# A feed-forward kernel: no plain feature tile, eighteen early P2 products, seven products for every tile

## The chip, the cores and the metric

The kernel runs on one core of one Trainium2 chip. Times are device microseconds (us) of that core. The engines are TensorE (PE: matmuls; PEld: its weight loads), VectorE (DVE), ScalarE (ACT), GpSimd (POOL) and the issuing queue of SyncE (SPq). SBUF and PSUM are the two memories on the core that the engines work on; the matmuls here write into PSUM, in banks. A "matmul" below is one instruction with a 128x128 stationary and a 128x512 moving operand, unless said otherwise.

## The reference

```
B, S, D, F = 32, 32, 1024, 3584          # 1024 tokens, bf16 throughout
def reference(x, w_gate, w_up, w_down):
    return (gelu_tanh(x @ w_gate) * (x @ w_up)) @ w_down
```

## The kernel before

The 3584 features are 28 feature tiles of 128, in 14 chunks of two. For one feature tile, the gate and up weights, each cut into the two halves of D, form a 2x2 block matrix (a11, a12: gate; a21, a22: up), and x transposed forms another (b11, b12: first half of D, tokens 0-511 and 512-1023; b21, b22: second half of D). A plain tile needs eight block products of four matmuls, 32 in all. Chunks 1 to 13 use a scheme of seven products (28 matmuls), which needs sums of blocks: s1 to s4 of the weights, per chunk, and t1 to t4 of x, once. The products P1 = a11 b11 and P2 = a12 b21 stay bf16; the other five multiply sums in fp32r, a 32-bit type. The last step of a tile is the gating product: VectorE multiplies gelu of the gate result by the up result.

- Before, chunk 0 is plain. Its 64 matmuls need no sums, and they fill PE while x arrives and VectorE forms the t's and the sums of chunk 1.
- P2 of ten further tiles is also made in the head ("ahead") from gate weights that arrive first, and kept in SBUF.
- GpSimd makes the sums of chunks 2 to 13. It starts when t4 is done.

```python
# head, before (cut)
for k in range(KQ):
    for j in range(KB):
        product_ahead(ps[j], 0, j, k, k + 1)      # P2 of tiles 2..5
plain0(KD, KD + KQ)                               # plain, tokens 0-511
...
tt(t1, b12, b11, SUB)                             # VectorE
for fl in range(FC):
    for which in (0, 1):
        plain(tok0[fl][which], which, fl, 0, 0, KD, KD, KD - 1)
    plain_out(fl, 0, *tok0[fl])
...
tt(t2, b22, t1, SUB)
chunk1 = sums(1, nc.vector)                       # s1, s2, s4 of chunk 1
...                                               # plain, tokens 512-1023
begun = [first_product(FC + fl) for fl in range(FC)]   # P1 of chunk 1

# one chunk (cut): order of the products on PE
for fl in range(FC): prod(psc[fl], s1[fl], t1, True);  sn5.append(snap(psc[fl], "sn5"))
for fl in range(FC): prod(psa[fl], s2[fl], t2, False); sn2.append(snap(psa[fl], "sn2"))
for st in open_fts:  last_product(st)             # a22 t4 of the chunk before; its gating
                                                  # product on VectorE frees that psA bank
for fl, ft in enumerate(fts):
    prod(psc[fl], s4[fl], b22r, False)
    h1.append(gelu(added(sn2[fl], psc[fl]), "h1", 2))   # this add frees the psC bank
begun = [first_product(ft + FC) for ft in fts]    # P1 of the next chunk, new psA banks
for fl, ft in enumerate(fts):
    prod(psa[fl], s3[fl], t3, False)
    tt(g_of(ft)[:, NB:], added(sn5[fl], psa[fl]), h1[fl], MUL)
```

`snap` copies a bank to SBUF on ScalarE, `added` adds on VectorE. There are eight PSUM banks: four psA, two psB, two psC.

Of the kernel before, what the change touches and what calls it, by code (L numbers as in the profile page):

```python
# [1 line left out]

# [11 lines left out]
def kernel(  # L14
# [20 lines left out]
    nc = tc.nc  # L35
    P = nc.NUM_PARTITIONS
# [14 lines left out]
    FC = 2  # L51
    NCH = FT // FC
    NAHEAD = 10
    KQ = DT // 4
# [12 lines left out]
    gpool = ctx.enter_context(tc.tile_pool(name="g", bufs=1))  # L67
    ring = ctx.enter_context(tc.tile_pool(name="ring", bufs=4))
    one = ctx.enter_context(ExitStack())
# [38 lines left out]

    a12_ahead = [ring.tile([P, KD, KB * P], bf16, name="a12a", tag="ring") for _ in range(2)]
    b11 = xpool.tile([P, KD, NB], bf16, name="b11")  # L110
    b21 = xpool.tile([P, KD, NB], bf16, name="b21")
    b12 = ring.tile([P, KD, NB], bf16, name="b12", tag="ring")
    b22 = ring.tile([P, KD, NB], bf16, name="b22", tag="ring")
    t1, t2, t3, t4, b22r = (xpool.tile([P, KD, NB], f32r, name=n) for n in ("t1", "t2", "t3", "t4", "b22r"))

    def x_rows(dt, nb):
        return ((b11, b12), (b21, b22))[dt // KD][nb][:, dt % KD, :]


    ahead = [  # L120
        gpool.tile([P, n, NB], fp32, name="ahead", tag=f"hi{n}", bufs=2) for n in (KB, KB, QF - KB)
    ]
    assert 2 * KB < NAHEAD <= KB + QF
    w_tiles = {}
# [15 lines left out]
    def quads(ci, fl=None):  # L140
        cols = slice(None) if fl is None else slice(fl * P, (fl + 1) * P)
        wg, wu = w_tiles[ci, 0], w_tiles[ci, 1]
        return wg[:, :KD, cols], wg[:, KD:, cols], wu[:, :KD, cols], wu[:, KD:, cols]

    s_tiles = {}

    def sums(ci, eng):

        a11, a12, a21, a22 = quads(ci)
        s1, s2, s4, s3 = (  # L150
            spool.tile([P, KD, FC * P], f32r, name=n, tag=n) for n in ("s1", "s2", "s4", "s3")
        )
        s_tiles[ci] = (s1, s2, s3, s4)
        yield eng.tensor_tensor(s1, a21, a22, ADD)  # L154
        yield eng.tensor_tensor(s2, s1, a11, SUB)  # L155
        yield eng.tensor_tensor(s4, a12, s2, SUB)  # L156
        yield eng.tensor_tensor(s3, a11, a21, SUB)  # L157

# [16 lines left out]
    with tc.manual_schedule():  # L175
        for eng, p0, p1 in ((nc.sync, 0, HALF), (nc.scalar, HALF, NB_P)):
# [3 lines left out]
            )  # L180
        alloc_w(0, 0)
        alloc_w(0, 1)

        def load_ahead(i, k0, k1):
            f0, n = FC + i * KB, min(KB, NAHEAD - i * KB)
            nc.sync.dma_start(  # L186
                out=a12_ahead[i][:, k0:k1, : n * P],
                in_=wg_r[:, KD + k0 : KD + k1, f0 * P : (f0 + n) * P],
            )

        def load_w0(eng, d0, d1):
            for which in (0, 1):
                load_w(eng, 0, which, d0, d1)

# [6 lines left out]
        for k in range(KQ):  # L201
            load_ahead(0, k, k + 1)
        load_w0(nc.scalar, KD, KD + KQ)
        load_xT(0, KD + KQ, DT)
        load_ahead(0, KQ, KD)
        load_w0(nc.sync, KD + KQ, DT)
        load_ahead(1, 0, KD)
        load_xT(0, 0, KD)
        load_w0(nc.sync, 0, KD)
        load_xT(1, 0, KD)  # L210
        load_xT(1, KD, DT)

        warm_ps = acc("A")
# [14 lines left out]

        def plain(ps, which, fl, nb, d0, d1, first=0, last=DT - 1):
            for dt in range(d0, d1):  # L230
                nc.tensor.matmul(  # L231
                    ps,
                    lhsT=w_tiles[0, which][:, dt, fl * P : (fl + 1) * P],
                    rhs=x_rows(dt, nb),
                    start=(dt == first),
                    stop=(dt == last),
                )

        def gelu(src, tag, bufs):
            h = ework.tile([P, NB], bf16, name=tag, tag=tag, bufs=bufs)  # L240
            nc.scalar.activation(h, src, ACT.Gelu_apprx_tanh)  # L241
            return h

        def plain_out(ft, nb, gate, up):
            tt(g_of(ft)[:, nb * NB : (nb + 1) * NB], gelu(gate, "h0", 4), up, MUL)  # L245

# [10 lines left out]

        def ahead_of(ft):
            i, j = divmod(ft - FC, KB)
            return ahead[i][:, j, :]  # L260

        def product_ahead(ps, i, j, k0=0, k1=KD):
            for k in range(k0, k1):
                nc.tensor.matmul(  # L264
                    ps,
                    lhsT=a12_ahead[i][:, k, j * P : (j + 1) * P],
                    rhs=b21[:, k, :],
                    start=(k == 0),
                    stop=(k == KD - 1),
                )  # L270


        ps = [acc(t) for t in "CCAA"]
        tok0 = [(acc("A"), acc("B")) for _ in range(FC)]

        def plain0(d0, d1):
            for which in (0, 1):
                for dt in range(d0, d1):
                    for fl in range(FC):
                        plain(tok0[fl][which], which, fl, 0, dt, dt + 1, KD, KD - 1)  # L280

        for k in range(KQ):
            for j in range(KB):
                product_ahead(ps[j], 0, j, k, k + 1)
        plain0(KD, KD + KQ)
        for j, copy in enumerate((nc.scalar.copy, nc.vector.tensor_copy) * 2):
            product_ahead(ps[j], 0, j, KQ)
            copy(ahead[0][:, j, :], ps[j])
        plain0(KD + KQ, DT)
        a12_ahead.append(ring.tile([P, KD, KB * P], bf16, name="a12a", tag="ring"))  # L290
        load_w_all(1, 1)
        load_w_all(1, 0)
        load_ahead(2, 0, KD)
        load_w_all(2, 0)
        for j, tag in enumerate("CCAA"):
            ps = acc(tag)
            product_ahead(ps, 1, j)
            (nc.scalar.copy, nc.vector.tensor_copy)[j % 2](ahead[1][:, j, :], ps)
        tt(t1, b12, b11, SUB)
        for fl in range(FC):  # L300
            for which in (0, 1):
                plain(tok0[fl][which], which, fl, 0, 0, KD, KD, KD - 1)
            plain_out(fl, 0, *tok0[fl])
        tok1 = [(acc("A"), acc("B")) for _ in range(FC)]
        for fl in range(FC):
            for which in (0, 1):
                plain(tok1[fl][which], which, fl, 1, 0, KD)
        tt(t2, b22, t1, SUB)
        nc.scalar.copy(b22r, b22)
        chunk1 = sums(1, nc.vector)  # L310
        for _ in range(3):
            next(chunk1)
        for fl in range(FC):
            for which in (0, 1):
                plain(tok1[fl][which], which, fl, 1, KD, DT)
            plain_out(fl, 1, *tok1[fl])
        load_w_all(2, 1)
        for j, tag in enumerate("CC"):
            ps = acc(tag)
            product_ahead(ps, 2, j)  # L320
            nc.scalar.copy(ahead[2][:, j, :], ps)

# [11 lines left out]
        def first_product(ft):  # L334
            psa = acc("A")
            prod(psa, quads(*divmod(ft, FC))[0], b11, True)
            if ft < FC + NAHEAD:
                return psa, gelu(added(ahead_of(ft), psa), "h0", 4)
            return psa, snap(psa, "sn1")
# [5 lines left out]

        tt(t3, b22, b12, SUB)
        begun = [first_product(FC + fl) for fl in range(FC)]
        next(chunk1)
# [3 lines left out]
        open_fts = []  # L352
        for ci in range(1, NCH):
            fts = range(ci * FC, (ci + 1) * FC)
            if fts[0] == HF:
                g_hi = g_tiles("hi", bf16, N)
            if ci + 1 < NCH:
                if ci + 2 < NCH:
                    load_w_all(ci + 2, 0)
                for _ in sums(ci + 1, nc.gpsimd):  # L360
                    pass
# [7 lines left out]
            for fl in range(FC):  # L369
                prod(psa[fl], s2[fl], t2, False)  # L370
                sn2.append(snap(psa[fl], "sn2"))
            for st in open_fts:
                last_product(st)
            for fl, ft in enumerate(fts):
                prod(psc[fl], s4[fl], b22r, False)
                h1.append(gelu(added(sn2[fl], psc[fl]), "h1", 2))
                a22r_of(ft)
            if ci + 2 < NCH:
                load_w_all(ci + 2, 1)

            if fts[0] < FC + NAHEAD:
                h0 = first
            else:
                for fl in range(FC):
                    psb = acc("B")
                    prod(psb, quads(ci, fl)[1], b21, True)
                    h0.append(gelu(added(first[fl], psb), "h0", 4))
            begun = [first_product(ft + FC) for ft in fts] if ci + 1 < NCH else []
            for fl, ft in enumerate(fts):
                prod(psa[fl], s3[fl], t3, False)  # L390
                tt(g_of(ft)[:, NB:], added(sn5[fl], psa[fl]), h1[fl], MUL)  # L391
            open_fts = list(zip(fts, psa, h0))

# [5 lines left out]
        NBT = len(batches)  # L399

        def load_b(f_off, col, b, t=None):
            k0, k1 = batches[b]
            if t is None:
                t = ring.tile([P, KB, NB], bf16, name="wdb", tag="ring")[:, : k1 - k0, :]
            nc.sync.dma_start(
                out=t, in_=wd_r[:, f_off + k0 : f_off + k1, col * NB : (col + 1) * NB]
            )
            return t
# [173 lines left out]
```

## Time and profile before

| | before |
|---|---|
| time, median of the 6 runs beside the result | 275.59 us |
| span of the profiled run | 273.7 us |
| PE busy | 269.1 us (98%) |
| PE idle after its start | one wait, 0.15 us |
| granted TensorE clock | 1.00 |
| last x quadrant (b22) landed (issue 14.89 + 4.2) | 19.1 us |
| first s1 product of chunk 2 | 38.54 us |

The first two lines are of the profile page: busy time of each engine, then the mean granted clock in 40 slices of the span (tenths; 9 is 90% or more), then the chain that ended last, by engine.

```profile
PE 269.1 (98%) x1199; PEld 187.9 (69%) x1199; DVE 195.9 (72%) x194; ACT 111.9 (41%) x183; POOL 107.3 (39%) x55
...
PEclk9999999999999999999999999999999999999999
...
PE 91%; SPq 5%; DMA 2%; issue 0%; DVE 0%; ACT 0%; DVEq 0%
```

The list of waits of PE (engine, line, what it waited for, us in total, times, longest):

```profile
PE psA L215 <- PEq L566: 0.8, 1, 0.8
PE psB L231 <- DVE lo L245: 0.2, 1, 0.2
```

PE is the limit from end to end, and it never waits for a load. The timeline of PE (start, duration, operation; bf16 products last about 1.73 us for eight matmuls from start to start, fp32r ones 1.815) at the end of the head and the beginning of chunk 2:

```profile
27.74 1.89 PE L249 MATMUL psA<-b,wg 128*128 128x512 bf16 x8
29.28 2.21 PE L249 MATMUL psC<-t,s 128*128 128x512 f32 x8
...
36.51 2.19 PE L249 MATMUL psA<-t,s 128*128 128x512 f32 x8
38.54 1.98 PE L249 MATMUL psC<-t,s 128*128 128x512 f32 x8
```

### The profile page before, as it was taken

Reading aid. Unit: us, or ns where it says so; the run is one execution under the profiler, and the core shown is the slowest. Engines: PE = TensorE matmul, PEld = TensorE weight load, DVE = VectorE, ACT = ScalarE, POOL = GpSimd, SP = SyncE. Lnnn points to the kernel's source line nnn. Section 1 sums busy time; section 2 is a strip of 40 time slices with the busy share of each in tenths; the row PEclk is TensorE's granted clock in tenths of the full one; section 3 lists DMA queues with packets and bytes.
Section 4 is the critical chain, followed back from the end, with each engine's and each line's share of the span. In section 5 each row is a group of like instructions: output and inputs, shape, how many; then the busy total and the mean of one; then the engine's idle time right before and its main releaser. Section 6 shows DMA issues by size and latency. Waiting matters only on the chain.

```text
span 273.7 us, 3347 instructions
## 1 busy us (share of the span) xinstructions
PE 269.1 (98%) x1199; PEld 187.9 (69%) x1199; DVE 195.9 (72%) x194; ACT 111.9 (41%) x183; POOL 107.3 (39%) x55
## 2 busy tenths in 40 slices
PE   8999999999999999999999999999999999999994
PEld 3444777877778676676868686754447888888883
DVE  0279986989756676676657556568999999999511
ACT  2262664553643646455563636430300023962001
POOL 1000099998797695949576675000000000000000
PEclk9999999999999999999999999999999999999999
DMA  7997532513505405050504280004992445686202
GB/s 175 267 245 198 152 104 50 156 54 102 156 8 145 135 18 153 3 153 0 156 25 130 67 282 0 0 2 161 353 292 79 116 153 172 230 279 202 78 0 78
DMA packets 55810, 35.08 MB, mean 128 GB/s; under 512 B 8689, under 2 KB 55793, under 8 KB 55793
## 3 DMA queue, kind: packets, MB, share of 16 engines
q1 hardware_dynamic: 52672, 32.38, 41.1%
q10 hardware_dynamic: 3120, 2.49, 2.7%
q8 instruction: 9, 0.15, 0.2%
q14 instruction: 9, 0.07, 0.1%
HBM read 30.93 MB, written 2.10 MB: 121 GB/s over the span
## 4 chain that ended last, share of the span: by engine, by line
PE 91%; SPq 5%; DMA 2%; issue 0%; DVE 0%; ACT 0%; DVEq 0%
PE psA L249 34%; PE psA L412 18%; PE psC L249 17%; PE psC L412 7%; PE psB L412 7%; PE psB L249 5%; SPq L197 3%; DMA b<-in_x_dram 2%; PE psB L231 1%; PE psA L231 1%; SPq L134 1%; SPq L186 1%; PE psC L264 1%; DVE lo L245 0%; ACT o_sb L552 0%
## 5 line engine op out<-in xcount | busy, mean ns | idle before, releaser
L249 PE MATMUL psA<-t,s 128*128 128x512 f32 x208 | 54.1, 402 | 0.0
L241 ACT ACTIVATE h<-c 128x512 bf16<-128x512 f32 x52 | 31.8, 628 | 37.2 <-DVE c L326 37.2
L249 PEld LDWEIGHTS psA<-t,s 128*128 128x128 f32 x208 | 39.1, 188 | 9.2
L154 POOL TENSOR_TENSOR s<-wu 128x1024 fp32r<-128x1024 bf16 x12 | 26.4, 2202 | 25.0 <-DMA wu<-in_w_up_dram 18.3
L326 DVE TENSOR_TENSOR c<-sn,psA 128x512 f32<-128x512 f32 x26 | 17.8, 683 | 16.8 <-PE psA L249 16.8
L249 PEld LDWEIGHTS <-wg 128*128 128x128 bf16 x168 | 15.4, 98 | 20.1 <-issue 3.4
L155 POOL TENSOR_TENSOR s<-s,wg 128x1024 fp32r<-128x1024 f32 x12 | 27.8, 2313 | 0.9
L156 POOL TENSOR_TENSOR s<-wg,s 128x1024 fp32r<-128x1024 bf16 x12 | 26.3, 2188 | 0.9
L157 POOL TENSOR_TENSOR s<-wg,wu 128x1024 fp32r<-128x1024 bf16 x12 | 26.6, 2213 | 0.0
L331 ACT COPY sn<-psC 128x512 f32<-128x512 f32 x26 | 15.2, 588 | 27.6 <-PE psC L249 23.8
L331 ACT COPY sn<-psA 128x512 f32<-128x512 f32 x42 | 23.6, 585 | 6.8 <-PE psA L249 6.8
L249 PE MATMUL psC<-t,s 128*128 128x512 f32 x104 | 25.9, 391 | 0.0
L249 PE MATMUL psA<-t,a22r 128*128 128x512 f32 x104 | 25.9, 391 | 0.0
L249 PE MATMUL psC<-b22r,s 128*128 128x512 f32 x104 | 25.7, 389 | 0.0
L249 PE MATMUL psA<-b,wg 128*128 128x512 bf16 x104 | 24.6, 380 | 0.0
L249 PEld LDWEIGHTS psC<-t,s 128*128 128x128 f32 x104 | 19.5, 188 | 4.2
L249 PEld LDWEIGHTS psA<-t,a22r 128*128 128x128 f32 x104 | 19.5, 188 | 4.1
L249 PEld LDWEIGHTS psC<-b22r,s 128*128 128x128 f32 x104 | 19.5, 188 | 4.1
L326 DVE TENSOR_TENSOR c<-sn,psC 128x512 f32<-128x512 f32 x26 | 17.9, 689 | 5.3 <-PE psC L249 5.3
L391 DVE TENSOR_TENSOR lo<-c,h 128x512 bf16<-128x512 f32 x12 | 19.2, 1602 | 0.6
L344 DVE TENSOR_TENSOR hi<-h,psA 128x512 bf16<-128x512 bf16 x14 | 9.6, 688 | 13.8 <-PE psA L249 13.8
L455 ACT COPY snb<-psC 128x512 f32<-128x512 f32 x4 | 2.2, 590 | 36.5 <-PE psC L412 36.5
(93 smaller groups left out, 402.6 us busy)
## 6 DMA issues: line engine op xcount, KB each, us to landing
wu<-in_w_up_dram SPq DMA_DIRECT2D x13, 512.0 KB, 4.0
wg<-in_w_gate_dram SPq DMA_DIRECT2D x13, 512.0 KB, 5.2
wdb<-in_w_down_dram SPq DMA_DIRECT2D x12, 512.0 KB, 4.7
wdb<-in_w_down_dram SPq DMA_DIRECT2D x12, 384.0 KB, 4.2
v<-in_w_down_dram SPq DMA_DIRECT2D x4, 512.0 KB, 6.2
out_dram<-o_sb ACTq DMA_DIRECT2D x16, 128.0 KB, 1.7
v<-in_w_down_dram SPq DMA_DIRECT2D x4, 384.0 KB, 7.5
a12a<-in_w_gate_dram SPq DMA_DIRECT2D x2, 256.0 KB, 5.9
```

Of the source, the lines that this page charges most:

```text
L154: yield eng.tensor_tensor(s1, a21, a22, ADD)
L155: yield eng.tensor_tensor(s2, s1, a11, SUB)
L156: yield eng.tensor_tensor(s4, a12, s2, SUB)
L157: yield eng.tensor_tensor(s3, a11, a21, SUB)
L197: nc.sync.dma_start_transpose(out=t[:, d0 % KD : (d1 - 1) % KD + 1, :], in_=xf[nb * NB : (nb + 1) * NB, d0 * P : d1 * P])
L241: nc.scalar.activation(h, src, ACT.Gelu_apprx_tanh)
L249: nc.tensor.matmul(ps, lhsT=lhs[:, k, :], rhs=rhs[:, k, :], start=(start and k == 0), stop=(k == KD - 1), skip_group_check=True,)
L326: tt(t, s, ps, ADD)
L331: nc.scalar.copy(t, ps)
L344: tt(g_of(ft)[:, :NB], h0, psa, MUL)
L391: tt(g_of(ft)[:, NB:], added(sn5[fl], psa[fl]), h1[fl], MUL)
L412: nc.tensor.matmul(banks[m], lhsT=lhs(k)[:, m * P : (m + 1) * P], rhs=rhs(k), start=(start and k == 0), stop=(k == HF - 1), skip_group_che ...
```

## The change

The intent is to drop the plain chunk: 56 matmuls in place of 64 for its two tiles. Something else must then fill PE while x and the first weights arrive, so P2 of eighteen tiles, not ten, is made in the head. The extra results are kept in SBUF slots that are needed later only. VectorE makes all sums of chunk 0 and s1 of chunk 1, GpSimd the rest. Because P1 of chunk 0 goes on accumulating in its bank before VectorE has time, ScalarE copies it to SBUF, and the add P1 + P2 of chunk 0 is put off into chunk 1.

```diff
-    NAHEAD = 10
+    NAHEAD = 18
-        load_w0(nc.sync, KD + KQ, DT)
-        load_ahead(1, 0, KD)
-        load_xT(0, 0, KD)
-        load_w0(nc.sync, 0, KD)
-        load_xT(1, 0, KD)
+        load_ahead(nc.sync, 1, KQ, KD)
+        load_ahead(nc.sync, 2, 0, KD)
+        load_xT(0, 0, KD)
+        load_ahead(nc.sync, 3, 0, KD)
+        load_xT(1, 0, KD)                 # b12
+        load_ahead(nc.sync, 4, 0, KD)
+        load_w_all(0, 1)                  # up weights of chunk 0
         load_xT(1, KD, DT)                # b22
+        load_w(nc.sync, 0, 0, 0, KD)      # gate weights of chunk 0, first half
 ... (plain0, plain, plain_out and their calls removed)
+        for ft in range(NAHEAD): ... product_ahead(ps, ft); copy(ahead[ft], ps)
+        chunk0 = sums(0, [nc.vector] * 4)
         tt(t1, b12, b11, SUB)
+        next(chunk0)                      # s1
         tt(t2, b22, t1, SUB)
+        next(chunk0); next(chunk0)        # s2, s4
+        tt(t3, b22, b12, SUB)
+        next(chunk0)                      # s3
-            if ft < FC + NAHEAD:
-                return psa, gelu(added(ahead_of(ft), psa), "h0", 4)
+            if FC <= ft < NAHEAD:
+                return psa, gelu(added(ahead[ft], psa), "h0", 4)
             return psa, snap(psa, "sn1")
-        for ci in range(1, NCH):
+        for ci in range(NCH):
+            if ci == 1:
+                open_fts = [(ft, ps, gelu(added(ahead[ft], p1), "h0", 4)) for ft, ps, p1 in open_fts]
             for st in open_fts:
                 last_product(st)
```

(The loop also loads the gate weights of chunk 2 a second time.)

More of the change, by code (lines that the diff above doesn't have):

```diff
@@ L1 @@
 from contextlib import ExitStack
+from itertools import cycle
 import concourse.bass as bass
@@ L67 @@
     gpool = ctx.enter_context(tc.tile_pool(name="g", bufs=1))
-    ring = ctx.enter_context(tc.tile_pool(name="ring", bufs=4))
+    ring = ctx.enter_context(tc.tile_pool(name="ring", bufs=2))
     one = ctx.enter_context(ExitStack())
@@ L105, in acc, with a12_tile @@
         return ps1.tile([P, NB], fp32, name=f"ps{tag}", tag=tag, bufs=BANKS[tag])
-    a12_ahead = [ring.tile([P, KD, KB * P], bf16, name="a12a", tag="ring") for _ in range(2)]
+    def a12_tile(pool, tag):
+        return pool.tile([P, KD, KB * P], bf16, name="a12a", tag=tag)
+    a12_ahead = [
+        a12_tile(*at) for at in ((spool, "s3"), (ring, "ra"), (ring, "ra"), (spool, "s2"), (spool, "s4"))
+    ]
     b11 = xpool.tile([P, KD, NB], bf16, name="b11")
     b21 = xpool.tile([P, KD, NB], bf16, name="b21")
-    b12 = ring.tile([P, KD, NB], bf16, name="b12", tag="ring")
-    b22 = ring.tile([P, KD, NB], bf16, name="b22", tag="ring")
+    b12 = ring.tile([P, KD, NB], bf16, name="b12", tag="rb")
+    b22 = ring.tile([P, KD, NB], bf16, name="b22", tag="rb")
     t1, t2, t3, t4, b22r = (xpool.tile([P, KD, NB], f32r, name=n) for n in ("t1", "t2", "t3", "t4", "b22r"))
@@ L117, in x_rows, with ahead_tile @@
         return ((b11, b12), (b21, b22))[dt // KD][nb][:, dt % KD, :]
-    ahead = [
-        gpool.tile([P, n, NB], fp32, name="ahead", tag=f"hi{n}", bufs=2) for n in (KB, KB, QF - KB)
-    ]
-    assert 2 * KB < NAHEAD <= KB + QF
+    def ahead_tile(pool, n, tag):
+        t = pool.tile([P, n, NB], fp32, name="ahead", tag=tag, bufs=2)
+        return [t[:, j, :] for j in range(n)]
+    ahead = [a for n in (KB, KB, QF - KB, QF - KB) for a in ahead_tile(gpool, n, f"hi{n}")]
     w_tiles = {}
@@ L142, in quads @@
         wg, wu = w_tiles[ci, 0], w_tiles[ci, 1]
-        return wg[:, :KD, cols], wg[:, KD:, cols], wu[:, :KD, cols], wu[:, KD:, cols]
+        a12 = wg[:, KD:, cols] if ci else a12_ahead[0][:, :, : FC * P][:, :, cols]
+        return wg[:, :KD, cols], a12, wu[:, :KD, cols], wu[:, KD:, cols]
     s_tiles = {}
@@ L153, in sums @@
         s_tiles[ci] = (s1, s2, s3, s4)
-        yield eng.tensor_tensor(s1, a21, a22, ADD)
-        yield eng.tensor_tensor(s2, s1, a11, SUB)
-        yield eng.tensor_tensor(s4, a12, s2, SUB)
-        yield eng.tensor_tensor(s3, a11, a21, SUB)
+        yield eng[0].tensor_tensor(s1, a21, a22, ADD)
+        yield eng[1].tensor_tensor(s2, s1, a11, SUB)
+        yield eng[2].tensor_tensor(s4, a12, s2, SUB)
+        yield eng[3].tensor_tensor(s3, a11, a21, SUB)
     a22rs = {}
@@ L180, with load_ahead @@
             )
-        alloc_w(0, 0)
-        alloc_w(0, 1)
-        def load_ahead(i, k0, k1):
-            f0, n = FC + i * KB, min(KB, NAHEAD - i * KB)
-            nc.sync.dma_start(
+        def load_ahead(eng, i, k0, k1):
+            f0, n = i * KB, min(KB, NAHEAD - i * KB)
+            eng.dma_start(
                 out=a12_ahead[i][:, k0:k1, : n * P],
@@ L189, in load_ahead @@
             )
-        def load_w0(eng, d0, d1):
-            for which in (0, 1):
-                load_w(eng, 0, which, d0, d1)
         def load_xT(nb, d0, d1):
@@ L201 @@
         for k in range(KQ):
-            load_ahead(0, k, k + 1)
-        load_w0(nc.scalar, KD, KD + KQ)
+            load_ahead(nc.sync, 0, k, k + 1)
+            load_ahead(nc.scalar, 1, k, k + 1)
         load_xT(0, KD + KQ, DT)
-        load_ahead(0, KQ, KD)
-        load_w0(nc.sync, KD + KQ, DT)
-        load_ahead(1, 0, KD)
+        load_ahead(nc.sync, 0, KQ, KD)
+        load_ahead(nc.sync, 1, KQ, KD)
+        load_ahead(nc.sync, 2, 0, KD)
         load_xT(0, 0, KD)
-        load_w0(nc.sync, 0, KD)
+        load_ahead(nc.sync, 3, 0, KD)
         load_xT(1, 0, KD)
+        load_ahead(nc.sync, 4, 0, KD)
+        load_w_all(0, 1)
         load_xT(1, KD, DT)
+        alloc_w(0, 0)
+        load_w(nc.sync, 0, 0, 0, KD)
+        load_w_all(1, 1)
+        load_w_all(1, 0)
+        load_w_all(2, 0)
         warm_ps = acc("A")
@@ L227 @@
         nc.tensor.matmul(warm_ps[:, : NB // 2], lhsT=ones_w, rhs=ones_m[:, : NB // 2], start=True, stop=True)
-        def plain(ps, which, fl, nb, d0, d1, first=0, last=DT - 1):
-            for dt in range(d0, d1):
-                nc.tensor.matmul(
-                    ps,
-                    lhsT=w_tiles[0, which][:, dt, fl * P : (fl + 1) * P],
-                    rhs=x_rows(dt, nb),
-                    start=(dt == first),
-                    stop=(dt == last),
-                )
         def gelu(src, tag, bufs):
@@ L242, in gelu @@
             return h
-        def plain_out(ft, nb, gate, up):
-            tt(g_of(ft)[:, nb * NB : (nb + 1) * NB], gelu(gate, "h0", 4), up, MUL)
         def prod(ps, lhs, rhs, start):
@@ L256, in prod, with product_ahead @@
                 )
-        def ahead_of(ft):
-            i, j = divmod(ft - FC, KB)
-            return ahead[i][:, j, :]
-        def product_ahead(ps, i, j, k0=0, k1=KD):
+        def product_ahead(ps, ft, k0=0, k1=KD):
+            i, j = divmod(ft, KB)
             for k in range(k0, k1):
@@ L270, in product_ahead @@
                 )
-        ps = [acc(t) for t in "CCAA"]
-        tok0 = [(acc("A"), acc("B")) for _ in range(FC)]
-        def plain0(d0, d1):
-            for which in (0, 1):
-                for dt in range(d0, d1):
-                    for fl in range(FC):
-                        plain(tok0[fl][which], which, fl, 0, dt, dt + 1, KD, KD - 1)
-        for k in range(KQ):
-            for j in range(KB):
-                product_ahead(ps[j], 0, j, k, k + 1)
-        plain0(KD, KD + KQ)
-        for j, copy in enumerate((nc.scalar.copy, nc.vector.tensor_copy) * 2):
-            product_ahead(ps[j], 0, j, KQ)
-            copy(ahead[0][:, j, :], ps[j])
@@ L289 @@
-        plain0(KD + KQ, DT)
-        a12_ahead.append(ring.tile([P, KD, KB * P], bf16, name="a12a", tag="ring"))
-        load_w_all(1, 1)
-        load_w_all(1, 0)
-        load_ahead(2, 0, KD)
-        load_w_all(2, 0)
-        for j, tag in enumerate("CCAA"):
-            ps = acc(tag)
-            product_ahead(ps, 1, j)
-            (nc.scalar.copy, nc.vector.tensor_copy)[j % 2](ahead[1][:, j, :], ps)
-        tt(t1, b12, b11, SUB)
-        for fl in range(FC):
-            for which in (0, 1):
-                plain(tok0[fl][which], which, fl, 0, 0, KD, KD, KD - 1)
-            plain_out(fl, 0, *tok0[fl])
@@ L304 @@
-        tok1 = [(acc("A"), acc("B")) for _ in range(FC)]
-        for fl in range(FC):
-            for which in (0, 1):
-                plain(tok1[fl][which], which, fl, 1, 0, KD)
+        head = [acc(t) for t in "CCBBAAAA"]
+        for q in range(2):
+            for k in range(KQ):
+                for ft in range(q * KB, (q + 1) * KB):
+                    product_ahead(head[ft], ft, k, k + 1)
+        for ft in range(NAHEAD):
+            if ft < 2 * KB:
+                ps = head[ft]
+                product_ahead(ps, ft, KQ)
+            else:
+                ps = acc("CCBBAAAA"[ft % 8])
+                product_ahead(ps, ft)
+            if ft == len(ahead):
+                ahead += ahead_tile(ring, 2, "ra")
+            (nc.vector.tensor_copy if ft % 3 == 1 and ft < 3 * KB else nc.scalar.copy)(ahead[ft], ps)
@@ L308 @@
+        chunk0 = sums(0, [nc.vector] * 4)
+        tt(t1, b12, b11, SUB)
+        next(chunk0)
         tt(t2, b22, t1, SUB)
         nc.scalar.copy(b22r, b22)
-        chunk1 = sums(1, nc.vector)
-        for _ in range(3):
-            next(chunk1)
-        for fl in range(FC):
-            for which in (0, 1):
-                plain(tok1[fl][which], which, fl, 1, KD, DT)
-            plain_out(fl, 1, *tok1[fl])
+        next(chunk0)
+        next(chunk0)
+        tt(t3, b22, b12, SUB)
+        next(chunk0)
@@ L317 @@
         load_w_all(2, 1)
-        for j, tag in enumerate("CC"):
-            ps = acc(tag)
-            product_ahead(ps, 2, j)
-            nc.scalar.copy(ahead[2][:, j, :], ps)
         def added(s, ps):
@@ L344, in last_product @@
             tt(g_of(ft)[:, :NB], h0, psa, MUL)
-        tt(t3, b22, b12, SUB)
-        begun = [first_product(FC + fl) for fl in range(FC)]
+        begun = [first_product(fl) for fl in range(FC)]
+        chunk1 = sums(1, (nc.vector, nc.gpsimd, nc.gpsimd, nc.gpsimd))
         next(chunk1)
@@ L359 @@
                     load_w_all(ci + 2, 0)
-                for _ in sums(ci + 1, nc.gpsimd):
+                for _ in chunk1 if ci == 0 else sums(ci + 1, [nc.gpsimd] * 4):
                     pass
@@ L377 @@
                 a22r_of(ft)
-            if ci + 2 < NCH:
+            if 0 < ci < NCH - 2:
                 load_w_all(ci + 2, 1)
-            if fts[0] < FC + NAHEAD:
+            if 0 < fts[0] < NAHEAD:
                 h0 = first
-            else:
+            elif ci:
                 for fl in range(FC):
@@ L391 @@
                 tt(g_of(ft)[:, NB:], added(sn5[fl], psa[fl]), h1[fl], MUL)
-            open_fts = list(zip(fts, psa, h0))
+            open_fts = list(zip(fts, psa, h0 or first))
         A11, A12 = [[g[:, :, :NB] for g in gs] for gs in (g_hi, g_lo)]
@@ L399 @@
         NBT = len(batches)
+        ring_tags = cycle(("ra", "rb"))
         def load_b(f_off, col, b, t=None):
@@ L403, in load_b @@
             if t is None:
-                t = ring.tile([P, KB, NB], bf16, name="wdb", tag="ring")[:, : k1 - k0, :]
+                t = ring.tile([P, KB, NB], bf16, name="wdb", tag=next(ring_tags))[:, : k1 - k0, :]
             nc.sync.dma_start(
```

## The prediction

> **What bounds it now.** TensorE: the page has PE busy 98% of 273.7 us, the chain of waits is 91% PE, and the list of waits shows PE idle once after its start (0.15 us at 19.98). The clock is 1.00 throughout. The head hides its loads only just: the DMA row is saturated from about 4 to 22 us.
>
> **Removed, added, moved.** Two plain tiles are 64 matmuls of 0.216 us; seven products each need 56, of which 40 are fp32r at 0.227 us. PE saves 1.73 - 0.44 = 1.3 us, with small start-up waits perhaps 1.6. P2 of eight more tiles only moves into the head. That is all the gain.
>
> **What it costs.** The plain tiles also hid the loads of x, wu and wg and DVE's preparation. By issue time plus time to landing (DMA view) the last x transpose (b22) landed at 19.1 us, with 4.0 MiB up to it. In the new order that is 4.75 MiB; at the 0.5 MiB per 1.8 to 2 us seen there it lands at T = 21.6, and wg of chunk 0, now behind it, at 22.5. (The Trainium skill, "DMA: Bandwidth & Descriptors", Specifications, has a higher fabric ceiling than this trace's 240 to 330 GB/s; I use the trace.)
>
> PE ends P2 of 18 tiles at 4.7 + 72 x 0.216 = 20.3 and idles about 2 us for wg.
>
> DVE then does in turn t2, s2, s4, t3, s3, s1 of chunk 1, t4 (2.29 us for 128x2048, 1.22 for 128x1024): 11.8 us after T. Only then come the adds that release psC (PE ready 1 us earlier) and GpSimd's sums for chunk 1. Eight adds of 0.69, two products of 1.6 to 1.9 (so long while GpSimd runs; the skill, "SBUF — State Buffer", tells of a port pair that the two lock in turn) and the first gating product follow before chunk 0's psA banks are free: T + 21.5, where PE wants them at T + 19.8. So three new PE waits: 2 us (DMA), 1 (DVE, psC), 0.5 to 2 (DVE, psA).
>
> Chunk 2 would start its s1 product at T + 24 to T + 25, about 46; before it was 38.54, with P2 of 6 tiles more (5.2 us) to do, so 43.7 compares. Net +1 to +3.5 us.
>
> Later I expect no change: the gate weights of chunk 2 are loaded twice, and each later gate load waits for a P2 two chunks before, but GpSimd had 3.4 us idle per chunk. The down projection is untouched.
>
> **Predicted:** 278.0 us, 8 in 10 within 275.2 to 280.3. Faster by over 2%: 0.01; within 2%: 0.95; slower by over 2%: 0.04.
>
> **What would show it.** Page: 8 matmuls fewer. PE waits: about 2 us at 20 us before chunk 0's first product (releaser DMA, wg), then DVE waits near 34 and 41 to 43 us (adds, gating product). DMA view: b22 landing near 21.6. DVE timeline: t4 ending near 33.5. Windows after 60 us: PE as dense as before.
>
> **What would make it wrong.** Earlier landing[...]: each microsecond of T is one of the result, and with b22 at 19.5 and short products the change is neutral. Or slack in the psA and psC waits that I mis-added; without them the gain nearly pays the DMA wait. On the other side: a late a12 tile stalling the head, or late GpSimd sums delayed by the weight loads.

## The result, and the profile after

| | before | after |
|---|---|---|
| time, median of 6 runs each | 275.59 us | 285.37 us |
| ratio | | 1.0353 [1.0328, 1.0378] |
| span of the profiled run | 273.7 us | 284.3 us |
| first s1 product of chunk 2 | 38.54 us | 54.23 us |
| from there to the end | 235.2 us | 230.1 us |

A ratio is the mean time of one kernel's fast runs over the mean of the other's in the same rounds, so it is not quite the ratio of the medians quoted beside it. The change is 3.5% slower: outside the predicted range, and past the 2% that the prediction gave a chance of 0.04.

The last row says where. After chunk 2 has started, the new kernel needs 5.1 us less, which is P2 of the six more tiles it has already done (6 x 4 x 0.216 = 5.2 us). So nothing is lost after that point; corrected for it, chunk 2 starts at 54.23 where before it would be 38.54 + 5.2 = 43.7, and these 10.5 us are the whole loss. (This is the profiled run, which was the slowest of its six at 286.14 us; the medians differ by 9.8 us.)

Page of the changed kernel, the same lines:

```profile
PE 270.3 (95%) x1175; PEld 191.7 (67%) x1191; DVE 197.1 (69%) x201; ACT 118.4 (42%) x193; POOL 112.5 (40%) x58
...
PEclk9999997799999999999999999999999999999999
...
PE 81%; SPq 5%; DVE 5%; issue 4%; DMA 3%; ACT 0%; DVEq 0%
```

PEld has 8 instructions fewer, as meant (some PE records are missing, so its own count is off). The clock row has a dip in the seventh and eighth slice. The waits of PE:

```profile
PE psA L246 <- DVE lo L313: 4.6, 1, 4.6
PE psA L246 <- DMA wg<-in_w_gate_dram: 3.3, 1, 3.3
PE psA L225 <- PEq L539: 0.8, 1, 0.8
PE psA L246 <- DVE c L295: 0.4, 1, 0.4
PE psC L246 <- DVE c L295: 0.4, 1, 0.4
PE psA L246 <- issue: 0.2, 1, 0.2
```

The timeline of PE, from the end of the head to chunk 2 (the bracket is idle time before, and its releaser):

```profile
18.88 1.89 PE L258 MATMUL psC<-b,a12a 128*128 128x512 bf16 x8
24.07 1.90 PE L246 MATMUL psA<-b,wg 128*128 128x512 bf16 x8 [3.31 <-DMA wg<-in_w_gate_dram]
25.62 2.20 PE L246 MATMUL psC<-t,s 128*128 128x512 f32 x8
...
41.69 1.99 PE L246 MATMUL psC<-b22r,s 128*128 128x512 f32 x8
48.28 1.01 PE L246 MATMUL psA<-b,wg 128*128 128x512 bf16 x2 [4.61 <-DVE lo L313]
49.51 2.34 PE L246 MATMUL psA<-b,wg 128*128 128x512 bf16 x5 [0.22 <-issue]
51.29 3.10 PE L246 MATMUL psA<-t,s 128*128 128x512 f32 x8
54.23 1.98 PE L246 MATMUL psC<-t,s 128*128 128x512 f32 x8
```

The places of the waits are those of the prediction: for wg of chunk 0 (its releaser is named), a small one near 35 us for the adds, and one near 43 us for the gating product. Their sizes are not. VectorE in the same stretch:

```profile
23.39 2.29 DVE L284 TENSOR_TENSOR t<-b,t 128x2048 fp32r<-128x2048 bf16 x1 [2.27 <-DMA b<-in_x_dram]
...
32.47 2.28 DVE L318 TENSOR_TENSOR t<-b,t 128x2048 fp32r<-128x2048 bf16 x1
34.67 1.27 DVE L295 TENSOR_TENSOR c<-sn,psC 128x512 f32<-128x512 f32 x2
35.87 1.27 DVE L295 TENSOR_TENSOR c<-ahead,psA 128x512 f32<-128x512 f32 x2
37.09 0.69 DVE L295 TENSOR_TENSOR c<-sn,psA 128x512 f32<-128x512 f32 x1
37.81 2.20 DVE L362 TENSOR_TENSOR lo<-c,h 128x512 bf16<-128x512 f32 x1
39.93 0.67 DVE L295 TENSOR_TENSOR c<-sn,psA 128x512 f32<-128x512 f32 x1
40.64 1.92 DVE L362 TENSOR_TENSOR lo<-c,h 128x512 bf16<-128x512 f32 x1
42.49 5.14 DVE L295 TENSOR_TENSOR c<-ahead,sn 128x512 f32<-128x512 f32 x2
47.55 1.46 DVE L313 TENSOR_TENSOR lo<-h,psA 128x512 bf16<-128x512 bf16 x2
```

The line to see is the one at 42.49. These are the two deferred adds P1 + P2 of chunk 0. The other adds of the same size take 0.69 us; these two take 5.14 us together. They differ in one thing: both operands are in SBUF (`ahead`, `sn`), while each other add has one in PSUM (`psA`, `psC`). GpSimd was busy all that time, with sums that read SBUF:

```profile
41.97 2.58 POOL L163 TENSOR_TENSOR s<-wu 128x1024 fp32r<-128x1024 bf16 x1
44.63 2.46 POOL L164 TENSOR_TENSOR s<-s,wg 128x1024 fp32r<-128x1024 f32 x1
47.16 2.47 POOL L165 TENSOR_TENSOR s<-wg,s 128x1024 fp32r<-128x1024 bf16 x1
```

The gating product that frees the psA bank (L313) stands behind the two adds.

The windows view of the changed kernel (columns: stretch, its length, busy time and instructions of each engine, then the granted clock, DMA share, GB/s):

```profile
43.60:48.20 4.60, 0.07 (x1) 0.01 (x1) 4.60 (x3) 1.17 (x2) 4.44 (x3) 0.80 0.13 32
48.20:53.20 5.00, 4.70 (x11) 2.58 (x12) 3.26 (x6) 3.33 (x7) 3.52 (x2) 0.50 0.03 3
53.20:54.20 1.00, 1.00 (x5) 0.81 (x5) 0.62 (x1) 0.11 (x1) 0.00 (x0) 0.99 0.60 156
```

After PE had been idle for 4.6 us it ran at half its clock for the next 5 us. From the end of the wait to the start of chunk 2 it took 5.95 us (48.28 to 54.23). The same products at full clock take 3.56 us, as in the run e8_psb_again below:

```profile
42.70 1.89 PE L246 MATMUL psA<-b,wg 128*128 128x512 bf16 x7 [0.92 <-DVE lo L314]
...
46.26 1.98 PE L246 MATMUL psC<-t,s 128*128 128x512 f32 x8
```

So in this profile the wait cost 2.4 us more than its own length.

So the theory, formed from the two traces: of the 10.5 us, 3.3 us are the wait for wg, 0.8 us small waits, 4.6 us the wait for the gating product, which would have been about 0.9 us had the two adds taken 0.69 us each, and 2.4 us the lowered clock. This is 11.1 us; the rest is what is left of the saved matmuls (1.3 us by count) after small gaps. Rivals: the adds are slow by themselves, or late for another reason; the clock fell for another reason; the second load of chunk 2's gate weights costs time.

### The profile page after: what moved, and what is told of

It reads as the page before. It is cut to its first block, busy times and chain, and to the rows that moved or that the text cites. A ratio compares the mean times of both kernels' runs of the same rounds, so it can differ in the third digit from the quotient of the medians.

```text
span 284.3 us, 3349 instructions
## 1 busy us (share of the span) xinstructions
PE 270.3 (95%) x1175; PEld 191.7 (67%) x1191; DVE 197.1 (69%) x201; ACT 118.4 (42%) x193; POOL 112.5 (40%) x58
## 4 chain that ended last, share of the span: by engine, by line
PE 81%; SPq 5%; DVE 5%; issue 4%; DMA 3%; ACT 0%; DVEq 0%
PE psA L246 32%; PE psA L385 18%; PE psC L246 15%; PE psC L385 7%; PE psB L385 7%; SPq L200 3%; PE psB L246 3%; DMA b<-in_x_dram 3%; DVE c L295 2%; SPq L193 1%; DVE t L288 1%; DVE s L165 0%; DVE s L164 0%; DVE t L318 0%; DVE lo L313 0%
## 5 line engine op out<-in xcount | busy, mean ns | idle before, releaser
L246 PE MATMUL psA<-t,s 128*128 128x512 f32 x224 | 59.3, 407 | 0.0
L241 ACT ACTIVATE h<-c 128x512 bf16<-128x512 f32 x56 | 34.4, 628 | 45.1 <-DVE c L295 45.1
L246 PEld LDWEIGHTS psA<-t,s 128*128 128x128 f32 x224 | 42.7, 191 | 10.5 <-issue 0.3
L246 PE MATMUL psA<-b,wg 128*128 128x512 bf16 x103 | 27.1, 396 | 8.5 <-DVE lo L313 4.6
L165 POOL TENSOR_TENSOR s<-wg,s 128x1024 fp32r<-128x1024 bf16 x13 | 28.3, 2180 | 1.0
L246 PE MATMUL psA<-t,a22r 128*128 128x512 f32 x112 | 28.2, 392 | 0.4 <-DVE c L295 0.4
L246 PE MATMUL psC<-t,s 128*128 128x512 f32 x112 | 28.0, 392 | 0.4 <-DVE c L295 0.4
L166 POOL TENSOR_TENSOR s<-wg,wu 128x1024 fp32r<-128x1024 bf16 x13 | 28.4, 2182 | 0.0
L246 PE MATMUL psC<-b22r,s 128*128 128x512 f32 x112 | 27.7, 389 | 0.0
L300 ACT COPY sn<-psC 128x512 f32<-128x512 f32 x28 | 16.5, 588 | 26.1 <-PE psC L246 23.3
L313 DVE TENSOR_TENSOR hi<-h,psA 128x512 bf16<-128x512 bf16 x14 | 9.6, 687 | 15.3 <-PE psA L246 15.3
L313 DVE TENSOR_TENSOR lo<-h,psA 128x512 bf16<-128x512 bf16 x14 | 9.6, 686 | 14.5 <-PE psA L246 14.4
```

Of the source, the lines that this page charges most:

```text
L165: yield eng[2].tensor_tensor(s4, a12, s2, SUB)
L166: yield eng[3].tensor_tensor(s3, a11, a21, SUB)
L241: nc.scalar.activation(h, src, ACT.Gelu_apprx_tanh)
L246: nc.tensor.matmul(ps, lhsT=lhs[:, k, :], rhs=rhs[:, k, :], start=(start and k == 0), stop=(k == KD - 1), skip_group_check=True,)
L300: nc.scalar.copy(t, ps)
L313: tt(g_of(ft)[:, :NB], h0, psa, MUL)
```

## The experiments

All kernels gave a right result except one. The diffs are shortened. e1 to e4 ran together, then e8, e5, e6 and e7, then e11, e12, e9 and e10, then e13 alone.

### e1_psb: the deferred adds read one operand from PSUM

P2 of tiles 0 and 1 is left in the two psB banks, which nothing else uses before chunk 9. Six banks serve the rest of the head.

```diff
-        head = [acc(t) for t in "CCBBAAAA"]
+        head = [acc(t) for t in "BBCCAAAA"]
-                ps = acc("CCBBAAAA"[ft % 8])
+                ps = acc("CCAAAA"[(ft - 2 * KB) % 6])
-            copy(ahead[ft], ps)
+            if ft >= FC:
+                copy(ahead[ft], ps)
-                open_fts = [(ft, ps, gelu(added(ahead[ft], p1), "h0", 4)) ...]
+                open_fts = [(ft, ps, gelu(added(p1, head[ft]), "h0", 4)) ...]
```

> Edit: P2 of feature tiles 0 and 1 stays in the two psB banks, and the two deferred adds read it there (one operand in PSUM) instead of an SBUF copy. Theory (the two deferred adds took 5.14 us together because both operands are in SBUF and GpSimd ran at the same time, and the PE wait that this made longer also cost the clock): the adds take about 0.69 us each, the PE wait on the gating product falls from 4.6 to about 0.9 us, the clock stays at 1.00, and the time falls by about 3.7 + 2.4 = 6 us to 279 us. Rival (the adds were slow or late for another reason, such as the order of work on VectorE or waiting for ScalarE): they stay long, time 284 to 286 us.

Measured: 278.62 us, ratio to before 1.0102 [1.0074, 1.013]. The same place on VectorE:

```profile
39.37 1.93 DVE L363 TENSOR_TENSOR lo<-c,h 128x512 bf16<-128x512 f32 x1
41.22 1.27 DVE L296 TENSOR_TENSOR c<-sn,psB 128x512 f32<-128x512 f32 x2
42.59 1.28 DVE L314 TENSOR_TENSOR lo<-h,psA 128x512 bf16<-128x512 bf16 x2
```

The two adds took 1.27 us in place of 5.14. The wait for the gating product was gone, and the time fell by about 6.7 us between the medians, the expected size. Two thirds of the loss are explained by where two small adds found their operand, with the clock that followed from their wait.

### e2_hold: the same operands, but GpSimd held back

```diff
-                for _ in chunk1 if ci == 0 else sums(ci + 1, [nc.gpsimd] * 4):
-                    pass
+                if ci != 1:
+                    for _ in chunk1 if ci == 0 else sums(ci + 1, [nc.gpsimd] * 4):
+                        pass
             if ci == 1:
                 open_fts = [...]                                   # the two deferred adds
+                nc.gpsimd.tensor_copy(ident[:, :1], open_fts[1][2][:, :1])
+                for _ in sums(ci + 1, [nc.gpsimd] * 4):
+                    pass
```

> Edit: the operands stay as in the changed kernel, but GpSimd's sums for chunk 2 are held back until after the two deferred adds. Theory (contention with GpSimd): each of the two adds takes about 0.69 us with both operands still in SBUF, the PE wait falls to about 1 us, clock 1.00, time about 279 us, as in the run with psB. Rival (adds of two SBUF operands of this type are slow by themselves): they stay at about 2.5 us each and the time stays at 284 to 286 us or rises.

Measured: 279.79 us, ratio 1.014 [1.0106, 1.0173]. The view of the tile `ahead` (duration in ns: least, median, most), first in the changed kernel:

```profile
L295 DVE TENSOR_TENSOR c<-ahead,psA x16: 674/687/689, 35.9 to 117.7; 128x512 f32<-128x512 f32 x16
...
L295 DVE TENSOR_TENSOR c<-ahead,sn x2: 2604/2611/2618, 42.5 to 45.0; 128x512 f32<-128x512 f32 x2
```

and in e2_hold:

```profile
L295 DVE TENSOR_TENSOR c<-ahead,psA x16: 679/689/689, 35.7 to 111.4; 128x512 f32<-128x512 f32 x16
...
L295 DVE TENSOR_TENSOR c<-ahead,sn x2: 679/680/680, 42.3 to 42.9; 128x512 f32<-128x512 f32 x2
```

The same instruction on the same operands takes 2611 ns with GpSimd at work and 680 ns without. In e2_hold GpSimd was idle from 41.8 to 44.3 us:

```profile
39.22 2.60 POOL L166 TENSOR_TENSOR s<-wg,wu 128x1024 fp32r<-128x1024 bf16 x1
44.29 0.19 POOL L344 COPY ident<-h 128x1 bf16<-128x1 bf16 x1 [2.48 <-ACT h L241]
```

So the adds are not slow by themselves. This is what the Trainium skill, "SBUF — State Buffer", section "Who interferes with whom", states: a VectorE instruction with two SBUF inputs contends with a GpSimd instruction that reads SBUF, and whichever starts first blocks the other for its whole instruction; one with at most one SBUF input (and not in one of VectorE's two-port modes) does not contend. This trace agrees: the blocked adds last about as long as one of GpSimd's sums (2.1 to 2.6 us), they end at about 45.1 and 47.6, each half a microsecond after a sum (44.55 and 47.09), and the 16 adds with a PSUM operand stay at 0.69 us with GpSimd running beside most of them.

### e3_fill: PE kept busy in the second wait

```diff
+            if ci == 1:
+                fill_ps = acc("B")
+                for _ in range(21):
+                    nc.tensor.matmul(fill_ps, lhsT=ones_w, rhs=ones_m, start=True, stop=True)
             begun = [first_product(ft + FC) for ft in fts] ...
```

> Edit: 21 matmuls of constants (0.216 us each, 4.5 us, into an unused bank) are put where PE waited 4.6 us, nothing else. Theory (the PE idle time itself lowered the granted clock): the clock stays at 1.00 from 40 to 60 us, the first product of chunk 2 and the s3 product after it take 3.55 us in place of 5.95, and the time falls by about 2.4 us to 283 us though no wait was removed. Rival (the clock fell for another reason, or costs nothing): time 285 us or more.

Measured: 283.77 us, ratio 1.0277 [1.0237, 1.0316], against 1.0353 for the changed kernel in its own rounds and 1.03 when that was run again (below). The windows view of e3_fill:

```profile
43.30:48.00 4.70, 4.64 (x22) 2.16 (x23) 4.60 (x5) 1.26 (x2) 4.54 (x3) 1.00 0.00 1
48.00:51.50 3.50, 3.50 (x18) 2.32 (x17) 3.02 (x5) 2.93 (x6) 2.59 (x2) 1.00 0.02 5
```

The gating product on VectorE, and PE after the fill:

```profile
46.41 1.46 DVE L313 TENSOR_TENSOR lo<-h,psA 128x512 bf16<-128x512 bf16 x2
...
47.94 1.89 PE L246 MATMUL psA<-b,wg 128*128 128x512 bf16 x8
...
51.49 1.98 PE L246 MATMUL psC<-t,s 128*128 128x512 f32 x8
```

The deferred adds still took 5.16 us, no wait was removed, and yet the clock stayed at 1.00 and the products from 47.94 to the start of chunk 2 at 51.49 took 3.55 us in place of 5.95. The saving in place is the expected 2.4 us, less 0.8: the fill was too long, for the bank was free at about 47.1 (46.41 + 0.69) and the constants ran until 47.94. In the medians the total gained 1.6 us on the first runs of the changed kernel and only 0.4 on its second runs (e11 below), with intervals that overlap and across chips, so the time alone does not settle it.

Nor is this one profile proof that idle time lowers the clock. In it the clock had fallen after the first wait (0.57 from 24 to 28 us); e11 fell there too and then kept 1.00 after an unfilled second wait of 3.9 us. The clocks of all runs say more: the mean clock was 0.988 or 0.994 in all 20 runs of the changed kernel and its e4/e12 version, and 1.000 in two of the four runs of e3_fill. The clearest pair is e10 and e13 below, without and with ten matmuls in the first wait: 0.991 to 0.993 in all four runs, and 0.998 to 1.000 in all six.

### e4_nodup and e12_nodup_again: without the second load of chunk 2's gate weights

```diff
-                if ci + 2 < NCH:
+                if 0 < ci and ci + 2 < NCH:
                     load_w_all(ci + 2, 0)
```

> Edit: the second, needless load of the gate weights of chunk 2 (512 KB) is left out, which also gives later gate loads a free slot earlier. Theory (it is off the critical path): within 0.4 us of the changed kernel, 285 us. Rival (the extra load and the later gate loads cost part of the 10 us): 1 us or more faster.

Measured: 284.42 us, ratio 1.0303 [1.0267, 1.034]. That is between the two theories, so it was run again beside the changed kernel.

> The changed kernel itself, run again on the same chip as the next three, for their comparison. Expected: 285 us, 3.5% slower than the kernel before.

Measured: 284.18 us, ratio 1.03 [1.0276, 1.0324], 1.2 us lower than the first time. In its profile the clock fell after the first wait (0.77 in the stretch 24 to 28 us), and the later wait was 3.9 us without a fall after it; in the first profile it was the other way round.

> e4_nodup again (without the second load of the gate weights of chunk 2), because its first result lay 1 us below that of the changed kernel, from different chips. Theory (off the critical path): within 0.5 us of e11_after_again. Rival (the extra load costs about 1 us): 0.8 us or more faster than e11_after_again.

Measured: 285.56 us, ratio 1.0352 [1.0335, 1.037]: here slower than the changed kernel by more than the intervals, in the first pair faster. No gain from leaving the load out can be seen; the difference of such pairs is within the spread that the clock and the landing of x bring.

### e8_psb_again: the base for the next three

> The same kernel as e1_psb, run again beside the next three so that they are compared on the same chip. Expected: 278.6 us as before, plus or minus 0.5, with a first PE wait of 2 to 3.5 us for the gate weights of chunk 0.

Measured: 279.36 us (278.16 to 279.52), ratio 1.0113 [1.0086, 1.0141]. In its profile the clock did not fall after the first wait (in that of e1_psb it did), and instead PE waited 0.9 us and 0.3 us for VectorE.

### e6_psb_late: the last x quadrant made to land later

```diff
         load_w_all(0, 1)
+        w_tiles[2, 0] = wpool.tile([P, DT, FC * P], bf16, name="wg", tag="wg", bufs=3)
+        load_w(nc.sync, 2, 0, 0, DT)          # 512 KB, moved up from below
         load_xT(1, KD, DT)                    # b22
```

> Edit on e1_psb: a 512 KB load (the first load of the gate weights of chunk 2, which is loaded again later anyway) is moved in front of the last x transpose, nothing else. It makes the last x quadrant and the gate weights of chunk 0 land about 1.9 us later. Theory of the prediction (each microsecond of that landing is one of the result): the first PE wait grows by 1.9 us and the time rises by 1.5 to 2 us (to about 280.5), or more if the longer wait also costs clock. Rival (the head has slack, the landing matters little): less than 0.7 us.

Measured: 280.16 us, ratio 1.0158 [1.0129, 1.0187], 0.8 us above e8_psb_again in the medians, 1.2 us in the means. Wait for wg: 3.9 us against 2.2. That lies between the two expectations and the intervals overlap, so in the time the effect is not clear of noise; the landing itself varies by more than one microsecond between runs (table below). The profiles differ by more (3.1 us), but they are the slowest of the four runs here and the fastest of the four of e8.

### e5_psb_fill1 and e7_psb_fill1_actt: clock and VectorE's chain

e5 fills part of the first wait of e1_psb; e7 also takes 4.6 us off VectorE's chain, with a wrong result (relative error 2.65). GpSimd's sums then start sooner too, at 30.5 us in place of 35.1.

```diff
# e5
+        fill_ps = acc("A")
+        for _ in range(10):
+            nc.tensor.matmul(fill_ps, lhsT=ones_w, rhs=ones_m, start=True, stop=True)
         begun = [first_product(fl) for fl in range(FC)]
# e7, in addition
+        nc.scalar.copy(t3, b12)
+        nc.scalar.copy(t4, b21)
-        tt(t3, b22, b12, SUB)
-        tt(t4, b21, t2, SUB)
-        nc.gpsimd.tensor_copy(ident[:, :1], t4[:, 0, :1])
+        nc.gpsimd.tensor_copy(ident[:, :1], s_tiles[1][0][:, 0, :1])
```

> Edit on e1_psb: ten matmuls of constants (2.2 us) in the first PE wait, before the first product of chunk 0. In the profile of e1_psb the clock fell to one half after that wait and the first product and part of the next ran slow, about 1.5 us. Theory A (that loss is hidden, because VectorE's chain of sums is what chunk 1 and the banks wait for next): the clock stays at 1.00 there, a new PE wait on VectorE of about 1.3 us appears before the first product of chunk 2, and the time changes by less than 0.5 us. Theory B (PE alone bounds the head): about 1.5 us faster, 277.1 us.

Measured: 280.25 us, ratio 1.0152 [1.0131, 1.0172]: no gain, even 0.9 us above e8. The clock was 1.00 in the head and PE waited for VectorE three times, 1.6 us together. But e8 had little clock to win back: three of its four runs have a mean clock of 1.000.

> Edit on e5_psb_fill1, with a wrong result on purpose: t3 and t4 are copies of b12 and b21 made on ScalarE instead of differences made on VectorE, which takes 4.6 us off VectorE's chain; GpSimd's start is tied to the end of VectorE's last sum as before. Theory A (VectorE's chain takes back what the clock gives): no PE wait after the first one, and about 1.3 to 1.5 us faster than e5_psb_fill1 and e1_psb, 277.2 us. Theory B (VectorE's chain does not matter once the two adds are short): same time as e5_psb_fill1 within 0.4 us.

Measured: 278.19 us, ratio 1.0078 [1.0056, 1.0101], 2.1 us below e5, with no wait for VectorE. Theory A holds in this pair.

### e9_psb_nodup, e10_psb_reorder, e13_reorder_fill1: the same with a right result

e9 is e1 without the needless load. e10 also reorders VectorE: the adds on psB come earlier, and two products that nothing waits for come later (with more buffers for the results held in between).

```diff
+            if ci == 0:
+                h0 = [gelu(added(first[fl], head[fl]), "h0", 4) for fl in range(FC)]
             for fl, ft in enumerate(fts):
                 prod(psa[fl], s3[fl], t3, False)
-                tt(g_of(ft)[:, NB:], added(sn5[fl], psa[fl]), h1[fl], MUL)
+                c5 = added(sn5[fl], psa[fl])
+                ... # chunk 0: held until after the adds that free psC in chunk 1
```

> e1_psb without the second load of the gate weights of chunk 2. Theory (chunk 2 starts 24.8 us after the last x quadrant lands, whatever else happens, and that landing varies between 21.4 and 23.5 us from run to run): 278.2 to 279.4 us as e1_psb, so no clear gain from the load. Rival: about 1 us faster than e1_psb, 277.7 us.

Measured: 279.0 us (278.07 to 281.57), ratio 1.0123 [1.009, 1.0156]: as e1_psb.

> Edit on e9_psb_nodup, with a right result: on VectorE the two adds that read psB come before the adds of the s3 product, and chunk 0's two last products wait until chunk 0's psA banks and chunk 1's psC banks are free, so that what PE waits for is no longer behind 4 us of other work. Theory (VectorE's chain sets the start of chunk 2): no PE wait on VectorE before the first product of chunk 2, which starts about 23 us after the last x quadrant has landed in place of 24.8, and the time falls by 1 to 2 us to about 277 us; still above the kernel before, because the wait for the gate weights of chunk 0 is untouched. Rival (VectorE's order does not matter): as e9_psb_nodup.

Measured: 279.78 us, ratio 1.0146 [1.0126, 1.0167]. The wait for the gating product is gone, but the expected gain did not come. In its profile the clock fell after the first wait (0.68 in the stretch 24 to 28 us), so PE itself was late. That left it open whether each of the two costs hides the other, or both are irrelevant. e13 puts e10's order and e5's ten matmuls together.

> e10_psb_reorder plus the ten matmuls of constants in the first PE wait, result right. Theory (two costs side by side, the lowered clock after the first wait and VectorE's chain, each hiding the other): clock 1.00, no PE wait on VectorE over 0.4 us, chunk 2 starts about 23 us after the last x quadrant landed, time about 1.5 us below e10_psb_reorder and near e7_psb_fill1_actt: 278.2 us, ratio to before 1.008. Rival: 279.5 us or more, ratio 1.013 or more, like e5_psb_fill1 and e10_psb_reorder.

Measured: 278.92 us, ratio 1.0097 [1.0076, 1.0119]; clock 1.00, one wait for VectorE of 0.36 us. The ratio is half a per cent below e10 and e5, with intervals that do not overlap, though the gain is nearer to 1.3 us than to 1.5. So the two costs stand side by side: e5 takes one away and e10 the other, and e13 with both gone is faster than either. Against the versions with neither edit (e1 1.0102, e8 1.0113, e9 1.0123) no gain is shown: the intervals overlap. One reason may be the landing of b22: it came at 23.3 to 23.6 us in the profiles of the three kernels with the ten matmuls, and at 21.5 to 22.3 in those of e1, e8, e9 and e10. Whether that is chance (the changed kernel, without these matmuls, had 23.4 and 23.8) or their doing, no run here shows. No version beat the kernel before, and nothing here pointed to one that would.

### One table for all runs

All columns are read from the profiles: the start of t2 on VectorE, which in each of these runs began when b22 landed; the start of the first s1 product of chunk 2 on PE; their difference; and the span less that start.

| run | b22 landed | chunk 2 starts | difference | rest |
|---|---|---|---|---|
| changed kernel | 23.39 | 54.23 | 30.8 | 230.1 |
| e11 (again) | 23.77 | 52.24 | 28.5 | 230.2 |
| e3_fill | 22.24 | 51.49 | 29.3 | 230.1 |
| e4 / e12 (no second load) | 22.66 / 22.84 | 52.78 / 53.76 | 30.1 / 30.9 | 230.0 / 230.0 |
| e1, e8 (adds from psB) | 22.12, 21.46 | 46.89, 46.26 | 24.8, 24.8 | 230.1, 230.1 |
| e2_hold | 23.19 | 47.96 | 24.8 | 230.1 |
| e5_psb_fill1 | 23.56 | 48.34 | 24.8 | 230.1 |
| e9_psb_nodup | 22.30 | 47.08 | 24.8 | 230.0 |
| e6_psb_late | 24.13 | 49.40 | 25.3 | 230.1 |
| e10_psb_reorder | 22.12 | 46.62 | 24.5 | 230.5 |
| e7, e13 (clock and chain) | 23.33, 23.32 | 46.27, 46.35 | 22.9, 23.0 | 230.1, 230.0 |

The rest is the same within half a microsecond. Once the adds are right, the difference is 24.8 us in five of the runs (of four kernels), with b22 anywhere from 21.46 to 23.56 us. In these profiles each microsecond of that landing is a microsecond of the result; the direct test, e6, was too small to show it in the time.

## Why the prediction was wrong

The prediction had the direction and the places of the waits; its range ended at 280.3 us and the result was 285.37. It put the start of chunk 2 at about 46 us, and the profile has 54.23.

| step, as the prediction put it | what the runs showed |
|---|---|
| "PE saves 1.73 - 0.44 = 1.3 us" | 8 weight loads fewer; the saving is too small to see alone |
| b22 "lands at T = 21.6" | 23.39 in the profile; 21.5 to 23.8 in the profiles of this load order: about 1.8 us short there |
| PE "idles about 2 us for wg" | 3.3 us |
| VectorE "11.8 us after T", t4 ending near 33.5 | t4 ended at 34.75, 11.4 us after T: right |
| "two products of 1.6 to 1.9" | 2.20 and 1.92 us |
| "Eight adds of 0.69" | six did; two took 2.61 us each, 3.8 us more. The step that failed |
| psC wait of 1 us, psA wait of 0.5 to 2 us | 0.4 us, and 4.6 us, because of those two adds |
| no word of the clock | at half after the 4.6 us wait, 2.4 us in this profile (none here in e11). The term that was missing |
| "Chunk 2 would start ... at T + 24 to T + 25" | T + 24.8 in the variants where the two adds are short; in part luck, since t4 came 0.4 us sooner than predicted and the two products took 4.1 us together, not 3.2 to 3.8 |
| "Later I expect no change" | right: the rest is 230.1 us, and the second load costs nothing that can be seen |

The three misses add up: 1.8 + 3.8 + 2.4 = 8.0 us, and 54.2 - 46 = 8.2 us. In the profile of e11, where the clock did not fall at this place, the first two suffice: 2.2 + 3.8 = 6.0 us, and 52.2 - 46 = 6.2 us.

The failed step is "Eight adds of 0.69". The prediction took the duration of the group of adds from the trace, where every one had a PSUM operand, and used it for two new adds of the same shape with both operands in SBUF. It even cited the page on the shared port pair, for the two products beside them, and did not ask of each of the ten instructions where its operands were. The experiments e1 (operand moved) and e2 (GpSimd held) show this cause from two sides. With the two adds short, e1_psb and e8_psb_again ran in 278.62 and 279.36 us, inside the predicted range.

The second step, the clock, followed from the first. A PE wait was counted at its length; in the first profile it was the length and another half, in that of e11 the length alone. What the prediction called "slack in the psA and psC waits that I mis-added" was the right place to doubt, with the wrong sign.

What the two edits leave: e13 is still 1% above the kernel before. That is consistent with the wait for wg of chunk 0 (1.5 us beside 2.2 us of fill there), which is longer than the matmuls saved; a version without that wait was not found, so this last part is inferred and not shown by a run.

## What to carry to other kernels

When a duration is taken from a trace for a new instruction, check that its operands are in the same memories and that the same engines run beside it: here the same add took 0.68 or 2.61 us. Count a wait of TensorE at more than its length when it is some microseconds long, because the clock may be at half for as long again: here 4.6 us of wait were followed by 5 us at half clock, though in e11 3.9 us were followed by none. And a "wasteful" block that needs no preparation, like the plain chunk, can be worth more than the arithmetic it costs where the preparation is what runs late.

## What the Trainium skill lacked or had wrong

- "TensorE: Matmul & The Clock Gate", Part 1, has the clock fall after at least one idle window of about 3.4 us, free-running. The half clock itself agrees (0.50 after the 4.6 us wait). That waits of 2.2 us (e8_psb_again), 3.3 us (the changed kernel) and 3.9 us (e11) were followed by no fall fits a free-running window. What does not fit that figure is that less idle time was enough: in e1_psb a wait of 2.1 us was followed by 0.50 for over 2 us.
- The same page advises against PE-idle gaps; it does not say that filling one with matmuls of constants keeps the clock. It did: e3_fill stayed at 1.00 through 4.7 us of them, and e13 at 0.998 to 1.000 in all six runs where e10, without them, had 0.991 to 0.993.
- "SBUF — State Buffer", "Who interferes with whom", agrees (2611 ns against 680 ns). It gives no size for a short VectorE operation that meets a chain of long GpSimd ones; here each add took 1.9 us more than its 0.68, a little less than one GpSimd sum (2.1 to 2.6 us).
- "DMA: Bandwidth & Descriptors" says nothing of the spread of a landing from run to run: with one load order b22 landed between 21.5 and 23.8 us in different profiles.
